# A written-out order of all queues replaced by another one, with four added dependencies of GpSimd on VectorE

## The chip, the core and the metric

The kernel runs on one core of one Trainium2 chip. Its time is the device time of one execution in microseconds (us), the median of the runs. The core has a matrix engine (TensorE, PE in the profile; its weight loads are PEld), a vector engine (VectorE, DVE), an engine for activation functions (ScalarE, ACT), a general engine (GpSimd, POOL) and a queue engine from which most transfers are started (SyncE, SP). Each engine works off its own list of instructions in order. Between engines an instruction waits on semaphores.

## The reference

```python
def attn(q, k, v, centroids):            # B=4, H=8, S=768, D=64; 16 centroids per head
    q_assign = argmax(normed(q) @ normed(centroids).T)      # a cluster for each query
    k_assign = argmax(normed(k) @ normed(centroids).T)      # and for each key
    mask = q_assign[:, :, :, None] == k_assign[:, :, None, :]
    scores = where(mask, (q @ k.T) / sqrt(D), -1e9)
    return softmax(scores) @ v
def moe(x, w_in, w_out, g_ln):           # x: 3072 x 512, w_in: 512 x 1024, w_out: 1024 x 512
    h = x @ w_in
    solu = h * softmax(h)
    ln = (solu - mean(solu)) / sqrt(var(solu) + 1e-6) * g_ln
    return ln @ w_out
out = moe(attn(...) as 3072 tokens x 512)
```

## The kernel before, in words

**Attention.** The tokens of q and k arrive by DMA (`ld`) and are turned so that the head's 64 dimensions lie on the partitions: for batch 0 by PE transposes with copies out of PSUM (`tp`, `xa`, `xt`), for batches 1 to 3 by transposes of VectorE (`xt`). Casts to bf16 (`ca`) write them into the operands `qbig` and `kbig`; casts of v are `cv`, blanks of `kbig` are `bl`. The clusters come from products with the centroids (`cl` on PE), which VectorE turns back (`tb`, line 479), reduces to a maximum (`mx`, line 489), compares with it (`oh`, line 493: 1 where the product is the maximum, else 0; its widest form has 768 columns and reads two tiles of SBUF) and turns again (`ot`, lines 500 and 505). Copies (`pl`, "place") write the rows so found as further contraction rows below q and k, so that a pair of one cluster gets a higher score and the exponential removes all others. Scores (`S`, line 641) come in 144 regions of 1024 columns, each of two halves; ScalarE exponentiates a region (`E`, line 651) into one of five tiles; `V` (line 663) multiplies with v and a column of ones into one PSUM bank (`ob`); `N` (lines 675 and 686) divides by that column on VectorE and writes x.

**FFN.** For each of 24 blocks f of 128 tokens: x is transposed (`tx`, a DMA; for the first and the last block `ptx` on PE with a copy), `h` (line 772) multiplies with w_in into two banks, `hm` (line 782, VectorE) copies out and keeps the maximum, `ex` (line 798) exponentiates, `u` (line 805) is the product h·e, on GpSimd or VectorE; `tu` transposes u (a DMA), `bn` and `ag` (lines 816, 821, 823) give its variance, `as` a small term of it, `al` (line 840, GpSimd) the factor alpha; `y` (line 844) multiplies with w_out into the one bank `mb`, `sc` (lines 856 on ScalarE, 858 on VectorE) scales it out with alpha and frees the bank for the next `y`, `ou` stores. `w_in` comes in four loads (`li`) with casts on GpSimd (`wi`, line 580); `lo`, `me`, `mf`, `ce` prepare w_out.

**Where the order comes from.** The kernel lists every step by name. The table `ORDER` is one list of all names; the steps are issued in that order, so that what stands in it for one engine is that engine's queue. The table `AWAY` names the engine of a step where it isn't the usual one. No scheduler moves anything afterwards; semaphores are put in for the data dependencies between engines. A name has the step, then its number: `S108.0` is the first half of region 108, `y10.0` the first quarter of block 10, `ca3.1.0.0` batch 3, pair 1, q, first half of the rows.

Of the kernel before, what the change touches and what calls it, by code (L numbers as in the profile page):

```python
# [23 lines left out]
""".split(), "ACT"))
AWAY.update(dict.fromkeys("""
    as0 as11 as14 as15 as17 as18 as19 as2 as22 as23 as4 as5 as9 bl1.2 bl3.0 ce0 ce2 ce4 km mk
    pl0.0.1.0.0 pl0.1.0.0 pl0.1.0.1 pl0.2.0.0 pl0.2.1.0 pl0.3.0.0 pl0.3.1.1 pl1.0.0.0
    pl1.2.0.0 pl2.0.0.0 pl2.0.0.1 pl2.0.1.1 pl2.2.0.0 pl3.0.0.1 pl3.2.0.1 pl3.2.1.0 sc0 sc1
    sc12 sc13 sc14 sc16 sc4 sc9
""".split(), "DVE"))  # L30
AWAY.update(dict.fromkeys("""
    ca0.0.0.0.0 ca0.0.0.0.1 ca0.0.0.1.0 ca0.0.0.1.1 ce1 ce3 pl0.0.1.1 u0.0 u1.0 u10.0 u11.0
    u12.0 u13.0 u15.0 u16.0 u17.0 u18.0 u19.0 u2.0 u21.0 u22.0 u3.0 u4.0 u5.0 u6.0 u7.0 u8.0
    u9.0
# [39 lines left out]
pl1.2.0.1 pl1.2.1.1 pl1.2.1.0 h4.0.1 as2 bl1.2 hm4.0 ag1 al0 u2.0 ca1.2.1.1 S53.0 S53.1 V33.0
V33.1 h4.1.0 xt2.0.0 sc0 h4.1.1 hm4.1 bn2.0 bn2.1 E52 E53 ex3.0 V34.0 S54.0 S54.1 S55.0 S55.1 E54
V34.1 V35.0 h5.0.0 h5.0.1 S56.0 S56.1 y1.0 E55 S57.0 S57.1 E56 cv1.2.0 V35.1 E57 y1.1 hm5.0 N15
tu2 ou0 ld2.2.0 ld2.2.1.0 ld2.2.1.1 y1.2 S58.0 S58.1 E58 h5.1.0 S59.0 S59.1 V36.0 V36.1 V37.0
V37.1 V38.0 S60.0 S60.1 h5.1.1 E59 E60 ex4.0 V38.1 y1.3 S61.0 S61.1 S62.0 S62.1 E61 E62 xt2.0.1
xt2.1.0 u3.0 ca2.0.0.1 ca2.0.0.0 al1 ag2 xt2.1.1 hm5.1 bn3.0 N16 bn3.1 cl2.1 cl2.0 tb2.1 ca1.3.1.0
cv1.2.1 ca1.3.0.0 as3 ag3 tb2.0 cv1.3.0 ca1.3.1.1 al2 u4.0 ca2.0.1.1 al3 ca2.1.0.0 ca2.1.1.0  # L80
cv1.3.1 V39.0 V39.1 S63.0 S63.1 S64.0 S64.1 V40.0 V40.1 sc1 V41.0 V41.1 y2.0 mx2.0 as4 N17 E63
S65.0 S65.1 E64 E65 y2.1 S66.0 S66.1 y2.2 y2.3 E66 tu3 tu4 ou1 ld2.2.1.2 ld2.2.1 S67.0 S67.1 V42.0
V42.1 S68.0 S68.1 V43.0 V43.1 sc2 oh2.0 ot2.0 N18 pl2.0.1.1 pl2.0.0.0 bn4.0 xt2.2.0 pl2.0.0.1
pl2.0.1.0 ca2.0.1.0 y3.0 E67 S69.0 S69.1 y3.1 ca2.2.0.1 bl2.0 E68 E69 S70.0 S70.1 E70 y3.2 V44.0
y3.3 V44.1 V45.0 S71.0 S71.1 S72.0 S72.1 V45.1 sc3 N19 tx6 y4.0 y4.1 E71 E72 S73.0 S73.1 E73 V46.0
# [12 lines left out]
ld3.2.0.0 ld3.2.0.1 ld3.2.0.2 ld3.2.0 tu7 ld3.2.1.0 ld3.2.1.1 ld3.2.1.2 ld3.2.1 bl2.2 al5 cv2.2.0
cv2.2.1 ca3.0.1.0 ca2.3.0.1 cl3.0 cl3.1 sc5 bn6.1 tb3.0 bn7.0 bn7.1 ag6 tb3.1 S93.1 S94.0 S94.1
V60.0 V60.1 V61.0 V61.1 y6.0 E93 E94 S95.0 S95.1 E95 h10.0.0 V62.0 V62.1 h10.0.1 h10.1.0 ex9.0  # L100
cv2.3.1 u8.0 S96.0 S96.1 E96 S97.0 N25 S97.1 E97 as7 y6.1 y6.2 V63.0 h10.1.1 as8 u9.0 ca3.0.0.1
ag7 bn8.0 hm10.0 S98.0 S98.1 S99.0 S99.1 h11.0.0 V63.1 V64.0 h11.0.1 E98 E99 S100.0 S100.1 E100
# [1252 lines left out]
```

## Time and profile before

| | |
|---|---|
| median of 3 runs | 222.03 us (221.85 to 222.12) |
| profiled execution | 222.33 us, its span 220.5 us |
| granted TensorE clock | 1.00 |
| busy: PE, ACT, DVE, POOL | 211.4, 192.8, 185.7, 158.8 us |
| HBM | 133 GB/s over the span |

A line of the profile gives the source line, engine, operation, output and input tiles and their shapes, then the count, the busy time in us and the mean of one in ns. The time after the second bar is how long the engine had been idle just before such instructions, and what ended it. "<-DVE y L858" means that the instruction's wait ended with that instruction of VectorE. In a timeline row the first two numbers are the start and the length. Some 1 to 3% of the matmul records are missing from the trace.

### The profile page before, as it was taken

Reading aid. Unit: us, or ns where it says so; the run is one execution under the profiler, and the core shown is the slowest. Engines: PE = TensorE matmul, PEld = TensorE weight load, DVE = VectorE, ACT = ScalarE, POOL = GpSimd, SP = SyncE. Lnnn points to the kernel's source line nnn. Section 1 sums busy time; section 2 is a strip of 40 time slices with the busy share of each in tenths; the row PEclk is TensorE's granted clock in tenths of the full one; section 3 lists DMA queues with packets and bytes.
Section 4 is the critical chain, followed back from the end, with each engine's and each line's share of the span. In section 5 each row is a group of like instructions: output and inputs, shape, how many; then the busy total and the mean of one; then the engine's idle time right before and its main releaser. Section 6 shows DMA issues by size and latency. Waiting matters only on the chain.

```text
span 220.5 us, 6292 instructions
## 1 busy us (share of the span) xinstructions
PE 211.4 (96%) x2401; PEld 148.9 (68%) x2431; DVE 185.7 (84%) x430; ACT 192.8 (87%) x245; POOL 158.8 (72%) x198
## 2 busy tenths in 40 slices
PE   7899999999999999999999999999999999999984
PEld 4567577677678776777677677666777767655442
DVE  3699979968999999896799999994888856989982
ACT  3799999999999998999999989999999888685362
POOL 3686969897898999549939997879889054456610
PEclk9999999999999999999999999999999999999999
DMA  5998999999999993999999981939584229777522
GB/s 199 394 402 259 189 175 300 126 154 259 164 154 169 190 188 62 174 248 210 153 225 162 180 184 38 171 92 209 151 173 90 72 64 168 154 120 170 163 94 100
DMA packets 120911, 38.33 MB, mean 174 GB/s; under 512 B 109993, under 2 KB 116401, under 8 KB 120881
## 3 DMA queue, kind: packets, MB, share of 16 engines
q1 hardware_dynamic: 120448, 37.40, 81.7%
q10 hardware_dynamic: 432, 0.52, 0.7%
q8 instruction: 19, 0.31, 0.6%
q14 instruction: 12, 0.09, 0.2%
HBM read 23.11 MB, written 6.29 MB: 133 GB/s over the span
## 4 chain that ended last, share of the span: by engine, by line
PE 72%; DVE 10%; DMA 6%; POOL 5%; issue 3%; ACT 2%; SPq 1%; DVEq 0%; ACTq 0%; POOLq 0%
PE sb L641 22%; PE hb L772 16%; PE mb L844 15%; PE ob L663 12%; DMA w_st<-in_moe_w_in_dram 4%; PE hb L470 3%; DMA raw<-in_q_dram 2%; DVE w_st L782 2%; PE hb L396 2%; DVE xt L421 2%; DVE bs L816 2%; POOL kbig L441 1%; PE mb L470 1%; POOL w_in_sb L580 1%; POOL v L556 1%
## 5 line engine op out<-in xcount | busy, mean ns | idle before, releaser
L651 ACT ACTIVATE e<-sb 128x1024 bf16<-128x1024 f32 x144 | 139.9, 1024 | 8.9 <-PE sb L641 8.1
L641 PE MATMUL sb<-qbig,kbig 80*128 80x256 bf16 (+3 forms) x648 | 83.8, 261 | 1.3 <-ACT e L651 1.0
L641 PEld LDWEIGHTS <-kbig 80*128 80x128 bf16 (+1 forms) x648 | 62.9, 119 | 25.4 <-issue 8.6
L805 POOL TENSOR_TENSOR u<-e_sb,w_st 128x1024 bf16<-128x1024 bf16 x21 | 45.1, 2145 | 20.0 <-ACT e_sb L798 13.3
L663 PEld LDWEIGHTS <-e 128*128 128x128 bf16 x1152 | 48.6, 97 | 10.4 <-DVE x L686 0.6
L663 PE MATMUL ob<-v,e 128*128 128x65 bf16 x1140 | 51.4, 193 | 0.2
L772 PE MATMUL hb<-w_in_sb,xT 128*128 128x512 bf16 x173 | 50.6, 379 | 0.9 <-POOL v L1323 0.3
L844 PE MATMUL mb<-w_out_c,uT 128*128 128x512 bf16 x165 | 45.5, 379 | 1.2 <-DVE y L858 0.4
L816 DVE BATCH_NORM_STATS2 bs<-u 128x6 f32<-128x512 bf16 x48 | 31.6, 680 | 1.1 <-POOL u L805 1.1
L798 ACT ACTIVATE e_sb<-w_st,nmax 128x1024 bf16<-128x1024 f32 (+1 forms) x25 | 27.8, 1113 | 3.2 <-DVE w_st L782 1.8
L439 POOL CAST qbig<-xt 64x768 bf16<-64x768 f32 (+1 forms) x31 | 25.7, 830 | 6.5 <-PE ob L663 2.7
L441 POOL TENSOR_SCALAR kbig<-xt 64x768 bf16<-64x768 f32 (+1 forms) x32 | 27.6, 865 | 2.4 <-DVE xt L409 0.8
L840 POOL TENSOR_TENSOR alpha<-var,halves 128x1 f32<-128x1 f32 x24 | 15.3, 638 | 12.6 <-DVE var L823 8.0
L421 DVE STREAM_TRANSPOSE xt<-raw 128x768 f32<-128x768 f32 x24 | 22.5, 959 | 0.1
L844 PEld LDWEIGHTS <-uT 128*128 128x128 bf16 x176 | 15.2, 97 | 10.2 <-issue 0.8
L772 PEld LDWEIGHTS <-xT 128*128 128x128 bf16 x192 | 15.8, 98 | 8.8 <-issue 0.6
L686 DVE TENSOR_TENSOR x<-ob,den 128x256 bf16<-128x256 f32 (+2 forms) x40 | 19.0, 474 | 1.4
L782 DVE TENSOR_SCALAR_CACHE_REDUCE w_st<-hb 128x512 f32<-128x512 f32 x24 | 16.3, 680 | 3.8 <-PE hb L772 3.7
L782 DVE TENSOR_SCALAR_CACHE_REDUCE w_st<-hb,nmax 128x512 f32<-128x512 f32 x24 | 17.8, 740 | 1.9 <-PE hb L772 1.5
L856 ACT ACTIVATE y<-mb,alpha 128x512 f32<-128x512 f32 x15 | 10.3, 685 | 6.5 <-POOL alpha L840 3.6
L675 DVE RECIPROCAL den<-ob 128x4 f32<-128x4 f32 (+2 forms) x40 | 7.1, 178 | 10.4 <-PE ob L663 10.1
L556 POOL CAST v<-vf 128x384 bf16<-128x384 f32 x22 | 10.9, 504 | 3.3 <-DMA vf<-in_v_dram 2.6
(109 smaller groups left out, 202.6 us busy)
## 6 DMA issues: line engine op xcount, KB each, us to landing
vf<-in_v_dram SPq DMA_DIRECT2D x16, 384.0 KB, 5.3
out_dram<-y SPq DMA_DIRECT2D x23, 256.0 KB, 2.5
...
```

What stands on the lines that cost most here:

```text
L421: nc.vector.transpose(xts[b, p, i][:], raw_of(b, p, i))
L439: (nc.vector if e == "DVE" else nc.gpsimd).tensor_copy(dst, src)
L441: (nc.vector if e == "DVE" else nc.gpsimd).tensor_scalar(dst, src, scalar1=inv_C, scalar2=1.0, op0=Alu.mult, op1=Alu.mult)
L641: nc.tensor.matmul(reg[:, c:c + wd], kb[u, pp, side_of(h), keys], qb[u, pp, side_of(h), su * P:su * P + wd])
L651: nc.scalar.activation(es[r][:, :w], src, Act.Exp, scale=exp_scale, bias=-exp_scale)
L663: nc.tensor.matmul(ops_of(group_of[n])[:, s, :VW], es[r][:, c0:c0 + P], v1[index[b, pair_of(h)] % R][:, side_of(h), kt, :VW], start=(kt == ...
L772: nc.tensor.matmul(hb[f2][:], xTs[f][:, dc, :], w_in_sb[:, dc, f2 * BANK:(f2 + 1) * BANK], start=(dc == 0), stop=(dc == n_dc - 1))
L782: nc.vector.tensor_scalar(ff[f, "h"][:, f2 * BANK:(f2 + 1) * BANK], hb[f2][:], scalar1=-1.0, scalar2=nmax[:, f2 - 1:f2] if f2 else 3.0e38, ...
L798: nc.scalar.activation(ff[f, "e"][:, cols(f, f2)], ff[f, "h"][:, cols(f, f2)], Act.Exp, bias=ff[f, "nmax"][:, n_ff2 - 1:], scale=-1.0, acc ...
L805: (nc.vector if e == "DVE" else nc.gpsimd).tensor_tensor(ff[f, "u"][:, cols(f, f2)], ff[f, "e"][:, cols(f, f2)], ff[f, "h"][:, cols(f, f2) ...
L816: nc.vector.bn_stats(ff[f, "bs"][:, f2, :], ff[f, "u"][:, f2 * BANK:(f2 + 1) * BANK])
L844: nc.tensor.matmul(y_of(f, x), ff[f, "uT"][:, fc, :], w_out_c[:, fc, parts_of(f, x)], start=(fc == 0), stop=(fc == n_fc - 1))
```

## The change

ORDER is another list of the same steps: the queue of every engine is in another order, those of the DMA queue too. AWAY moves some steps to another engine: seven from GpSimd to ScalarE, eleven from ScalarE to GpSimd, 24 from VectorE to GpSimd (u14.0 and u20.0 among them), 20 from GpSimd to VectorE (u10.0, u13.0, u16.0, bl1.0 and bl3.2 among them), pl0.1.1.1, sc3, sc11 and sc15 from ScalarE to VectorE, pl3.2.1.0, sc12, sc13, sc14 and sc16 the other way. What each step computes, the tiles and the number of PE instructions stay. `BEHIND` is new: a step of GpSimd waits until a step of VectorE has ended, though no data pass between them.

```diff
 AWAY.update(dict.fromkeys("""
-    ca0.0.1.1.0 ca0.2.0.1 ca1.0.0.1 ca3.1.1.0 ca3.2.0.1 cv0.0.1 cv0.1.0 cv0.2.1 cv1.2.0
...
+    ca0.0.1.0.0 ca0.2.0.1 ca1.0.0.1 cv0.1.0 cv0.1.1 cv0.2.0 cv1.2.0 cv2.0.1 cv3.0.0 cv3.1.1
...
 """.split(), "ACT"))
...
 ORDER = """
...
-V46.1 S74.0 S74.1 E74 y4.2 y4.3 V47.0 lv2.0 ou2 ld3.0.0.0 lv2.1 tx8 lv2.2 ex5.0 V47.1 S75.0 S75.1
...
+V45.1 y4.1 E70 E71 S72.0 S72.1 E72 S73.0 S73.1 bn4.0 N19 V46.0 V46.1 V47.0 V47.1 bn4.1 y4.2 S74.0
...
 """.split()
+BEHIND = dict(x.split(":") for x in """
+    al3:oh2.0 al5:oh2.2 u9.0:oh3.0 ca3.1.0.0:oh3.2
+""".split())
...
-    def run(self):
-        done, holder = set(), {}
+    def run(self, tc):
+        done, holder, last = set(), {}, {}
         for name in ORDER:
...
+            block = tc.nc.cur_bb.bb
+            n = len(block.instructions)
             o["fn"]()
+            if name in BEHIND or name in BEHIND.values():
+                new = list(block.instructions)[n:]
+                last[name] = new[-1].name
+            if name in BEHIND:
+                tc.add_manual_dep(new[0], last[BEHIND[name]], mybir.DependencyInfo(
+                    mybir.DependencyClass.Sync, mybir.DependencyReason.DATA), reason="behind")
             done.add(name)
```

All lines of the steps have numbers higher by 13 after the change, in the rows below too.

VectorE, around sc1, the copy of the second y block (`y` from `mb`), before; `bs` are bn3.0 and bn3.1, `cst` tb2.1 and tb2.0, `mv` and `var` ag3, `den` and `x` N16:

```order
L782 TENSOR_SCALAR w_st_1504,nmax_1505<-hb1_93,nmax_1505 128x512
L816 BN_STATS bs_1611<-u_1598 128x6
L675 RECIPROCAL den_1613<-ob_94 128x6
L686 TENSOR_TENSOR x_1185<-ob_94,den_1613 128x6x64
L816 BN_STATS bs_1611<-u_1598 128x6
L479 STREAM_TRANSPOSE cst_1625<-hb1_93 128x384
L821 BN_AGGR mv_1632<-bs_1611 128x2
L823 TENSOR_SCALAR var_1634<-es6_1630,esum_1444,mv_1632 128x1
L479 STREAM_TRANSPOSE cst_1625<-hb0_92 128x384
L858 TENSOR_SCALAR y_1681<-mb_95,alpha_1602 128x512
```

The same place after the change (`mv` and `var` ahead of N16 are ag2):

```order
L795 TENSOR_SCALAR w_st_1496,nmax_1497<-hb1_93,nmax_1497 128x512
L834 BN_AGGR mv_1615<-bs_1428 128x2
L836 TENSOR_SCALAR var_1617<-es6_1302,esum_1273,mv_1615 128x1
L688 RECIPROCAL den_1619<-ob_94 128x6
L699 TENSOR_TENSOR x_1190<-ob_94,den_1619 128x6x64
L871 TENSOR_SCALAR y_1622<-mb_95,alpha_1432 128x512
L848 TENSOR_SCALAR es6_1670<-esum_1410 128x1
L829 BN_STATS bs_1506<-u_1435 128x6
```

sc1 stands directly behind N16; bn3.1, both tb and ag3 have moved behind it.

VectorE around sc9, before: it follows N30, bn10.1 and ot3.2.

```order
L675 RECIPROCAL den_2912<-ob_94 128x6
L686 TENSOR_TENSOR x_2911<-ob_94,den_2912 128x6x64
L816 BN_STATS bs_2730<-u_2716 128x6
L500 STREAM_TRANSPOSE oht_2990<-oh_2850 128x768
L858 TENSOR_SCALAR y_2992<-mb_95,alpha_2780 128x512
```

After (the first row is hm14.0, `es6` as12, the memset bl3.2, `bs` bn11.0 and bn11.1, the `mv` ag9, ag10 and ag11):

```order
L795 TENSOR_SCALAR w_st_2908,nmax_2909<-hb0_92 128x512
L848 TENSOR_SCALAR es6_2911<-esum_2875 128x1
L556 MEMSET kbig1_100 16x2x384
L829 BN_STATS bs_2929<-u_2902 128x6 x2
L834 BN_AGGR mv_2932<-bs_2807 128x2
L836 TENSOR_SCALAR var_2934<-es6_2630,esum_2434,mv_2932 128x1
L834 BN_AGGR mv_2938<-bs_2812 128x2
L836 TENSOR_SCALAR var_2940<-es6_2783,esum_2708,mv_2938 128x1
L834 BN_AGGR mv_2947<-bs_2929 128x2
L836 TENSOR_SCALAR var_2949<-es6_2900,esum_2777,mv_2947 128x1
L829 BN_STATS bs_2951<-u_2915 128x6
L871 TENSOR_SCALAR y_3027<-mb_95,alpha_2936 128x512
```

ot3.2 stands further ahead now, and nine instructions of the statistics and a memset stand between hm14.0 and sc9.

GpSimd after the change, from u9.0 on (the first row; its wait on DVE is that for oh3.0); behind it ca3.1.1.1, ca3.0.0.0, al6, pl3.0.1.1, pl3.0.0.1, ca3.1.1.0, cv3.0.1, ca3.0.1.0, pl3.0.0.0, al7 and al8, and after these rows as9 and pl3.0.1.0, the last that S108.0 needs:

```order
L818 TENSOR_TENSOR u_2500<-e_sb_2435,w_st_2247 128x1024 [waits DMAHW5_49,DVE_49,Activation_49]
L454 TENSOR_SCALAR kbig0_99<-xt_2258 64x768 [waits PE_49,Pool_49]
L452 CAST qbig0_96<-xt_2252 64x768
L853 TENSOR_TENSOR alpha_2504<-var_2491,halves_126 128x1 [waits Pool_49]
L544 COPY kbig0_99<-oht_2509 32x4x192 [waits DVE_49,Pool_49]
L544 COPY qbig0_96<-oht_2509 32x4x192
L454 TENSOR_SCALAR kbig0_99<-xt_2258 64x768 [waits Pool_49]
L569 CAST v1_0_102<-vf_2269 128x6x64 [waits DMAHW5_49]
L454 TENSOR_SCALAR kbig0_99<-xt_2254 64x768
L544 COPY qbig0_96<-oht_2509 32x4x192 [waits Pool_49]
L853 TENSOR_TENSOR alpha_2626<-var_2608,halves_126 128x1 [waits DVE_49,Pool_49]
L853 TENSOR_TENSOR alpha_2628<-var_2618,halves_126 128x1 [waits DVE_49]
```

The same place before: u9.0 is the fourth row, and the placings (L531) come later.

```order
L805 TENSOR_TENSOR u_2442<-e_sb_2314,w_st_2099 128x1024 [waits DMAHW6_49,Activation_49]
L835 TENSOR_SCALAR es6_2459<-esum_2143 128x1
L835 TENSOR_SCALAR es6_2473<-esum_2313 128x1
L805 TENSOR_TENSOR u_2475<-e_sb_2439,w_st_2305 128x1024 [waits DMAHW0_49,DVE_49,Activation_49]
L439 CAST qbig0_96<-xt_2308 64x768 [waits PE_49,Pool_49]
L840 TENSOR_TENSOR alpha_2541<-var_2375,halves_126 128x1 [waits DVE_49,Pool_49]
L556 CAST v1_5_107<-vf_2330 128x6x64
L439 CAST qbig0_96<-xt_2321 64x768 [waits PE_49,Pool_49]
L840 TENSOR_TENSOR alpha_2545<-var_2480,halves_126 128x1 [waits DVE_49,Pool_49]
L439 CAST qbig0_96<-xt_2308 64x768
L441 TENSOR_SCALAR kbig0_99<-xt_2319 64x768 [waits Pool_49]
L531 COPY qbig0_96<-oht_2607 32x4x192 [waits DVE_49]
```

The first placing stands eight rows behind u9.0 before and four rows behind it after, and u9.0 has the wait for oh3.0 now.

VectorE in the tail, before, from hm21.0 to N39 (`u` is u20.0, the `bs` bn19.1, bn20.0, bn20.1):

```order
L782 TENSOR_SCALAR w_st_3779,nmax_3780<-hb0_92 128x512
L782 TENSOR_SCALAR w_st_3779,nmax_3780<-hb1_93,nmax_3780 128x512
L821 BN_AGGR mv_3783<-bs_3626 128x2
L823 TENSOR_SCALAR var_3785<-es6_3715,esum_3582,mv_3783 128x1
L805 TENSOR_TENSOR u_3800<-e_sb_3744,w_st_3717 128x1024
L816 BN_STATS bs_3752<-u_3681 128x6
L816 BN_STATS bs_3807<-u_3800 128x6 x2
L675 RECIPROCAL den_3810<-ob_94 128x2
L686 TENSOR_TENSOR x_2911<-ob_94,den_3810 128x128
```

After:

```order
L795 TENSOR_SCALAR w_st_3780,nmax_3781<-hb0_92 128x512
L795 TENSOR_SCALAR w_st_3780,nmax_3781<-hb1_93,nmax_3781 128x512
L829 BN_STATS bs_3799<-u_3670 128x6
L848 TENSOR_SCALAR es6_3801<-esum_3733 128x1
L829 BN_STATS bs_3799<-u_3670 128x6
L829 BN_STATS bs_3826<-u_3821 128x6 x2
L688 RECIPROCAL den_3829<-ob_94 128x2
L699 TENSOR_TENSOR x_2893<-ob_94,den_3829 128x128
```

u20.0 and ag18 are gone from between; bn19.0 has come behind hm21.1.

More of the change, by code (lines that the diff above doesn't have):

```diff
@@ L24 @@
 """.split(), "ACT"))
 AWAY.update(dict.fromkeys("""
[L26 to L29, printed above, removed]
+    as1 as10 as12 as13 as15 as16 as17 as20 as23 as3 as5 as6 as7 as8 bl1.0 bl1.2 bl3.2 ce0 ce2
+    ce4 km mk pl0.0.1.0.0 pl0.0.1.1.0 pl0.1.1.1 pl0.2.1.1 pl0.3.0.0 pl0.3.1.1 pl1.0.0.1
@@ L74 @@
[L74 to L85, printed above, removed]
@@ L98 @@
[L98 to L102, printed above, removed]
-V64.1 V65.0 V65.1 mx3.0 al6 cv2.3.0 ca3.1.0.1 al7 ca3.0.0.0 ca3.0.1.1 hm10.1 h11.1.0 oh3.0 hm11.0
@@ new lines @@
+S110.0 S110.1 V70.1 V71.0 V71.1 E109 E110 ex11.0 hm12.0 as10 oh3.2 y8.0 h12.1.1 y8.1 ca3.3.0.1
+bl3.0 ca3.3.1.0 S111.0 S111.1 S112.0 S112.1 N29 bn9.0 bn9.1 u10.0 bn10.0 hm12.1 bn10.1 y8.2 y8.3
+V72.0 V72.1 V73.0 h13.0.0 E111 E112 S113.0 S113.1 S114.0 S114.1 V73.1 h13.0.1 h13.1.0 h13.1.1
+V74.0 ot3.2 cv3.1.1 sc8 ex12.0 E113 hm13.0 V74.1 y9.0 h14.0.0 N30 hm13.1 ca3.1.0.1 ca3.1.0.0 as11
+u11.0 h14.0.1 E114 hm14.0 as12 pl3.2.1.0 pl3.2.1.1 u12.0 ca3.3.0.0 tu10 ou7 tx16 lv3.2 ou8 tu11
+bl3.2 bn11.0 bn11.1 ag9 al9 ag10 al10 pl3.2.0.0 cv3.1.0 ca3.2.0.0 ag11 bn12.0 ca3.2.1.0 ca3.2.1.1
@@ new lines @@
+h21.0.1 y17.0 y17.1 y17.2 hm20.1 ex20.0 S141.0 S141.1 E141 h21.1.0 y17.3 S142.0 S142.1 h21.1.1
+S143.0 S143.1 sc17 as18 ag18 as19 al18 hm21.0 hm21.1 E142 E143 ex21.0 y18.0 V94.0 bn19.0 as20
+y18.1 V94.1 y18.2 h22.0.0 h22.0.1 y18.3 sc18 u20.0 u21.0 bn19.1 bn20.0 bn20.1 N39 ag19 ag20 hm22.0
+h22.1.0 V95.0 V95.1 h22.1.1 hm22.1 ex22.0 al19 as21 u22.0 y19.0 ptx23.0 tx23.0 N40 y19.1 y19.2
+y19.3 ptx23.1 h23.0.0 h23.1.0 ou17 tu20 ou18 tu21 bn21.0 tx23.1 bn21.1 al20 h23.0.1 sc19 y20.0
+y20.1 y20.2 y20.3 sc20 h23.1.1 ou19 hm23.0 ag21 bn22.0 hm23.1 ptu22.0 ptu22.1 tu22.1 bn22.1 ex23.0
```

187 lines of the change are left out of this document (97 added, 90 removed).

## The prediction

> **What bounds the kernel now.** I read the page first, then the busy times by stage, then the waits, then the chain that ended last, and last the single stretches in which TensorE (PE) stands still.
>
> ```profile
> span 220.5 us, 6292 instructions
> PE 211.4 (96%) x2401; PEld 148.9 (68%) x2431; DVE 185.7 (84%) x430; ACT 192.8 (87%) x245; POOL 158.8 (72%) x198
> 0.00:14.00 14.00, 12.07 (x79) 7.39 (x80) 7.90 (x29) 8.70 (x18) 7.92 (x30) 1.00 0.87 318
> 14.00:44.00 30.00, 28.57 (x383) 20.07 (x383) 26.88 (x54) 29.32 (x36) 24.35 (x33) 1.00 1.00 226
> 44.00:204.00 160.00, 158.13 (x1861) 114.73 (x1886) 139.56 (x316) 147.71 (x181) 121.57 (x131) 1.00 0.84 157
> 204.00:221.00 17.00, 12.63 (x87) 6.75 (x85) 11.38 (x34) 7.08 (x14) 4.98 (x7) 1.00 0.36 116
> ```
>
> The stage rows give length, then the busy time of PE, PEld, DVE, ACT and POOL. From 44 to 204 us PE is busy 158.13 of 160 us: 1.87 us can be won there, and anything that makes PE wait is lost. From 14 to 44 us ACT stands beside it (29.32 of 30). The clock is 1.00 throughout, so nothing is won there.
>
> ```profile
> L641 PE MATMUL sb<-qbig,kbig 80*128 80x256 bf16 (+3 forms) x648 | 83.8, 261 | 1.3 <-ACT e L651 1.0
> ACT e L651 <- PE sb L641: 8.1, 19, 1.1
> 108.14 1.43 PE hb L470 x16
> 161.03 0.88 PE sb L641 x8
> 208.14 1.74 PE mb L844 x8
> ```
>
> PE waits 1.0 us in all for ACT's exponentials, ACT waits 8.1 us for PE's scores: PE leads. Three steps of the chain that ended last, from middle to end, say the same: they are PE work. PE's instructions are as many after the change as before, so the time is decided by the few gaps of PE that go, come or grow. The sum is made against the profiled execution, 222.33 us (span 220.5 and 1.8 around it), which lies 0.30 above the median of 222.03; I take 0.30 off at the end.
>
> **The change part by part.** First the gaps that go.
>
> ```profile
> 84.83 0.89 PE L663 MATMUL ob<-v,e 128*128 128x65 bf16 x24
> 85.32 0.71 DVE L858 TENSOR_SCALAR y<-mb,alpha 128x512 f32<-128x512 f32 x1
> 86.08 0.38 PE L844 MATMUL mb<-w_out_c,uT 128*128 128x512 bf16 x1 [0.36 <-DVE y L858]
> L816 DVE BATCH_NORM_STATS2 bs<-u 128x6 f32<-128x512 bf16 x48 | 31.6, 680 | 1.1 <-POOL u L805 1.1
> L479 DVE STREAM_TRANSPOSE cst<-hb 128x384 f32<-128x384 f32 x12 | 6.8, 577 | 0.5 <-PE hb L470 0.2
> L821 DVE BATCH_NORM_AGGREGATE mv<-bs 128x2 f32<-128x12 f32 x24 | 4.7, 195 | 0.1
> L823 DVE TENSOR_SCALAR var<-es,esum,mv 128x1 f32<-128x1 f32 x23 | 6.3, 273 | 1.4
> ```
>
> T1. There is one PSUM bank for y, so y2.0 waits for sc1, the copy of y1: 0.36 us by the row, about 0.5 against PE's usual start-to-start spacing. Between N16 and sc1 DVE now does bn3.1, two tb and ag3; after the change sc1 stands directly behind N16. By the rows 0.68 + 2×0.58 + 0.20 + 0.27 = about 2 us earlier. PE also has 6.0 us of work between y1.3 and y2.0 instead of 4.4 (two S halves, two V and two h more). The gap goes: −0.45 (0 to −0.5).
>
> ```profile
> 41.72 1.04 POOL L580 CAST w_in_sb<-w_st 128x1024 bf16<-128x1024 f32 x1 [0.80 <-DMA w_st<-in_moe_w_in_dram]
> 41.89 0.59 PE L772 MATMUL hb<-w_in_sb,xT 128*128 128x512 bf16 x2
> 42.81 0.38 PE L772 MATMUL hb<-w_in_sb,xT 128*128 128x512 bf16 x1 [0.33 <-POOL v L1323]
> 10.37 0.88 PE L396 MATMUL hb<-ident_f,raw 128*128 128x128 f32 x6 [0.26 <-ACT v L554]
> ```
>
> T2. h0.0.1 waits for the last cast of w_in on GpSimd (41.72 to 42.76), which waits for its DMA. The same bytes are queued ahead of that DMA afterwards, so I let it land at the same time; one V group (0.18 us) is put between on PE: −0.25 (0 to −0.5). T3. At the start the loads of pair 2 go ahead of the first load of v, and the wait at 10.37 goes; the next transpose then waits for ACT's copy xt0.1.0 instead: −0.1 (0 to −0.3).
>
> Now the gaps that come. All durations on DVE are means of the groups, less 0.08 for each neighbour, because successive vector instructions overlap (three statistics take 1.87, not 3×0.68).
>
> ```profile
> 201.02 1.87 DVE L816 BATCH_NORM_STATS2 bs<-u 128x6 f32<-128x512 bf16 x3
> L782 DVE TENSOR_SCALAR_CACHE_REDUCE w_st<-hb,nmax 128x512 f32<-128x512 f32 x24 | 17.8, 740 | 1.9 <-PE hb L772 1.5
> L858 DVE TENSOR_SCALAR y<-mb,alpha 128x512 f32<-128x512 f32 x8 | 5.9, 736 | 1.8 <-POOL alpha L840 1.2 <-PE mb L844 0.7
> L500 DVE STREAM_TRANSPOSE oht<-oh 128x768 bf16<-128x768 bf16 x6 | 5.8, 971 | 0.1
> 199.88 1.22 DVE L805 TENSOR_TENSOR u<-e_sb,w_st 128x1024 bf16<-128x1024 bf16 x1
> 205.40 0.29 DVE L686 TENSOR_TENSOR x<-sb,den 128x128 bf16<-128x128 f32 x1
> 205.98 0.22 PE L747 MATMUL sb<-ident_b,x 128*128 128x128 bf16 x1
> ```
>
> T4. y10.0 waits for sc9. Before, sc9 stands behind ot3.2; now behind bl3.2, bn11.0, bn11.1, ag9, ag10, ag11 and bn12.0, and u10.0 (1.22) has come to DVE ahead of it. From hm12.0 through sc9 I sum on DVE: five hm 3.2, oh and ot 1.9, two N 1.4, seven bn 4.2, u 1.1, three ag 1.35, bl and as 0.8, sc 0.7 = 14.7 us; plus 0.5 in which hm14.0 must wait for its matmuls. PE has 15.15 us of work from h12.0.1 to y10.0 (20 S halves at 0.22, 14 V at 0.18, 19 h and y at 0.43). That is even, so semaphore steps decide: +0.25 (0 to 0.7, one bn).
>
> T5. In the tail ptx23.1 needs N40. Before, N40 ends at 205.69 and ptx23.1 starts at 205.98: no wait. Afterwards DVE does between h21.1.1 and the end of N40: hm21.1 0.7, four bn 2.4, as 0.1, N39 0.4, two ag 0.9, two hm 1.3, tx23.0 0.3, N40 0.5, and links, 6.7 us; PE has 6.5. u20.0 is on GpSimd now (2.15 for 1.22), and bn20.0 may wait for it. +0.25 (0 to 0.85). T6. cl3.3 waits for the last of four DVE transposes, now behind hm11.1: +0.15 (0 to 0.7, one hm).
>
> T7. ACT gets lighter.
>
> ```profile
> L437 ACT ACTIVATE qbig<-xt 64x768 bf16<-64x768 f32 x3 | 2.5, 842 | 0.1
> L554 ACT CAST v<-vf 128x384 bf16<-128x384 f32 x10 | 5.1, 512 | 0.1
> L856 ACT ACTIVATE y<-mb,alpha 128x512 f32<-128x512 f32 x15 | 10.3, 685 | 6.5 <-POOL alpha L840 3.6 <-PE mb L844 2.9
> ```
>
> Two whole casts and two casts of v fewer (2×0.84 + 2×0.51), one copy of y more (0.69): −2.0 us on ACT. Nearly all of it lies after E25, where PE leads, so it is hidden behind PE; it can only take from the 1.0 us in which PE waits for E. I take −0.3 (0 to −1.0). DVE changes by about −2.8, GpSimd by about +5.3, mostly beside PE work.
>
> **The four dependencies.** Each holds a GpSimd step until a wide compare (oh) of VectorE has ended.
>
> ```profile
> 86.90 0.55 POOL L840 TENSOR_TENSOR alpha<-var,halves 128x1 f32<-128x1 f32 x1
> 87.40 0.82 POOL L439 CAST qbig<-xt 64x768 bf16<-64x768 f32 x1
> 87.56 1.48 DVE L493 TENSOR_TENSOR oh<-cst,mx 128x768 bf16<-128x768 f32 x1
> 88.19 1.53 POOL L441 TENSOR_SCALAR kbig<-xt 64x768 bf16<-64x768 f32 x1
> 111.78 0.95 DVE L493 TENSOR_TENSOR oh<-cst,mx 128x768 bf16<-128x768 f32 x1
> L805 POOL TENSOR_TENSOR u<-e_sb,w_st 128x1024 bf16<-128x1024 bf16 x21 | 45.1, 2145 | 20.0 <-ACT e_sb L798 13.3 <-issue 5.6 <-DVE y L858 0.6
> L441 POOL TENSOR_SCALAR kbig<-xt 64x768 bf16<-64x768 f32 (+1 forms) x32 | 27.6, 865 | 2.4 <-DVE xt L409 0.8
> L531 POOL COPY kbig<-oht 32x768 f32<-32x768 f32 (+2 forms) x14 | 10.0, 712 | 2.4 <-DVE oht L505 1.0 <-PE sb L641 0.5 <-DVE oht L500 0.3
> ```
>
> The compare at 87.56 began under a cast of GpSimd and took 1.48 us, one without it took 0.95; the next cast began under the compare and took 1.53 instead of 0.82. So one collision costs each side 0.5 to 0.7 us. The Trainium skill ("SBUF — State Buffer", section "SBUF: two separate sides") calls this an exclusive lock: a vector operation with two SBUF inputs or a GpSimd operation, whichever starts first, keeps the port pair for the whole instruction. The trace agrees (0.53 lost with 0.66 of the cast left). By that rule alone a u9.0 that began just before oh3.0 would hold it for about 2 us, and the dependencies would be a gain of that size on DVE, none of it on PE while slack remains.
>
> By the rows: u9.0 could begin about 1.8 us before oh3.0 ends and is held so long. Queued behind it on GpSimd up to S108.0 are four casts (3.4), al6, al7, al8 (0.55 each), four placings (3.3), a cast of v (0.5), an as (0.2), with u9.0 itself 2.15: 11.1 us. PE has about 12.1 us from the end of oh3.0 to S108.0. One microsecond is spare: 0 in the forecast (0 to +1.2). The al3 before S72.0 has about as much; al5 and ca3.1.0.0 more.
>
> Sum: −0.45 −0.25 −0.1 +0.25 +0.25 +0.15 −0.3 = −0.45, so 222.33 − 0.45 − 0.30 = 221.6. The tail from y20.0 on (12.5 us) keeps its two structural waits and its length.
>
> **The rivals.** A, the forecast: gains and new waits nearly cancel, 221.0 to 222.2; 0.39.
>
> B, the small waits of PE go almost everywhere. For it: ACT is 2 us lighter, and PE idles 1.87 us from 44 to 204 and 1.43 from 14 to 44. Against it: from E0 to E25 ACT's sum is unchanged. T1 to T3 at their ends (−1.3), half of what else is idle after 44 (−0.5), T4 to T6 at zero: 222.03 − 1.8 = 220.2 at best, 220.7 likely; 0.18.
>
> C, slower: GpSimd becomes late in one place, u9.0 to S108.0. It decides when oh3.0 ends over 1 us later than I sum, or two of the thirteen steps queued there run into wide vector operations at 0.5 to 0.7 each. For it: GpSimd carries 5 us more, and the wait puts a whole u behind DVE's clock. Then S108.0 stops PE for 0.5 to 1.5 us, and E behind it: 221.6 + 1.0 = 222.6, up to 223.4; 0.25.
>
> D, PE is not full. The Trainium skill ("Perfetto Trace Analysis", section "Identifying the Most-Contended Engine") calls matmul busy time a bad measure of headroom and takes weight-load time; here that is 68%, below ACT's 87%. As a mechanism here: the matmuls would close up wherever ACT frees a bank earlier, and the time would follow ACT's −2.0: 220.0. Against it stands ACT's 8.1 us of waits for PE; 0.06.
>
> E, slower: DVE is late at both sc9 and N40 (T4 and T5 at their upper ends, +1.05 over the forecast): 222.6; 0.12.
>
> **How the numbers follow.** 221.6 is that of A. The range holds A, most of B, C and E: 220.4 to 223.4. A measurement of this kernel can tell about 0.2% (0.44 us) from no change: faster means below 221.59, slower above 222.47. A is split evenly: 0.20 faster, 0.19 the same. With B and D faster has 0.44; same 0.19; slower 0.37 from C and E.
>
> **What would show it.** Right: y2.0 and h0.0.1 without idle time before them; y10.0 and ptx23.1 idle at most 0.5 us, with DVE named; S108.0 without a wait; oh3.0 and oh2.0 near 0.95 us. Wrong: S72.0 or S108.0 waiting for a GpSimd copy (C); y10.0 or ptx23.1 late by 0.7 or more (E); PE busy above 159 of 160 us in the middle (B); or a stall at a place not named here, which would mean that my sums of the queues miss a wait.

## The result, and the profile after

The changed kernel takes 223.41 us (median, 223.08 to 224.36) where the kernel before takes 222.03 (221.43 to 222.16): ratio 1.0072, 95% interval 1.0053 to 1.0091. It is slower by 0.7%, just above the forecast range. The trace below is of an execution of 223.08 us, 0.75 longer than the profiled one of before.

The page and the busy times by stage of the changed kernel (length, then PE, PEld, DVE, ACT, POOL):

```profile
span 221.3 us, 6294 instructions
PE 213.2 (96%) x2431; PEld 147.8 (67%) x2431; DVE 182.0 (82%) x425; ACT 191.0 (86%) x242; POOL 160.7 (73%) x206
0.00:14.00 14.00, 11.43 (x79) 6.69 (x80) 7.66 (x28) 8.38 (x17) 8.53 (x30) 1.00 0.89 312
14.00:44.00 30.00, 28.98 (x400) 20.50 (x399) 26.86 (x54) 29.21 (x35) 26.44 (x35) 1.00 0.98 241
44.00:204.00 160.00, 159.48 (x1866) 113.52 (x1865) 135.42 (x309) 146.01 (x178) 119.00 (x134) 1.00 0.83 155
```

ACT and DVE got lighter, about as worked out (192.8 to 191.0, 185.7 to 182.0); GpSimd rose by 1.9 us and not by 5.3. But PE is busier in the middle than before and the kernel is slower: busy shares don't settle this. The count in brackets says why. Here PE has as many matmul records as weight loads (2431); before it had 2401 (1.2% fewer), so some of its 1.87 us of "idle" in the middle were records that the trace had lost.

What works is to follow PE's delay: the start of a PE step, less the sum of the usual start-to-start spacings of all PE steps ahead of it in the queue (half of a region S 0.216 us, V 0.182, h and y 0.432, cl 0.77). The sum of the spacings is the "PE work done". The delay grows where PE really waits. It also grows a little where spacings are slightly above the usual ones (0.4 us from 48 to 78, with no wait of note), so columns are to be compared with each other. Growth per stretch, in us, worked out from the PE rows of four traces; "again" and "mended" are runs told of below:

| us of PE work done | before | changed | changed again | mended | what waits |
|---|---|---|---|---|---|
| 0 to 12 | 3.05 | 3.06 | 2.99 | 2.92 | the start |
| 12 to 24 | 0.94 | 0.60 | 0.60 | 0.60 | S behind E |
| 24 to 30 | 1.63 | 1.59 | 2.37 | 1.59 | S behind E; ptx0, cl1.0 |
| 30 to 36 | 0.84 | 0.59 | 0.52 | 0.58 | before: h0.0.1 (T2) |
| 36 to 48 | 0.16 | 0.98 | 0.98 | 0.39 | cl1.2 |
| 48 to 78 | 0.38 | 0.41 | 0.41 | 0.61 | |
| 78 to 84 | 0.55 | 0.02 | 0.01 | 0.02 | before: y2.0 (T1) |
| 84 to 144 | 0.40 | 0.30 | 0.31 | 0.31 | cl3.3 (T6) |
| 144 to 150 | 0.05 | 0.95 | 0.94 | 0.11 | S118.0, y10.0 (T4) |
| 150 to 192 | 0.19 | 0.18 | 0.35 | 0.37 | |
| 192 to 198 | 0.01 | 0.34 | 0.35 | 0.00 | ptx23.1 (T5) |
| 198 to the end | 1.13 | 1.06 | 1.06 | 1.06 | the tail |
| sum | 9.33 | 10.08 | 10.89 | 8.56 | |

The two gains that were forecast came: y2.0 and h0.0.1 start without a wait in the changed kernel's timeline, right behind the rows ahead of them.

```profile
42.19 0.35 PE L676 MATMUL ob<-v,e 128*128 128x65 bf16 x6
42.38 0.59 PE L785 MATMUL hb<-w_in_sb,xT 128*128 128x512 bf16 x2
...
84.03 0.50 PE L676 MATMUL ob<-v,e 128*128 128x65 bf16 x11
84.37 0.59 PE L857 MATMUL mb<-w_out_c,uT 128*128 128x512 bf16 x2
```

Waits that before did not have, at three places, took more than that back. The first place, in the timeline of the changed kernel around cl1.2 (L483):

```profile
51.50 0.43 DVE L699 TENSOR_TENSOR x<-ob,den 128x256 bf16<-128x256 f32 x1
52.14 0.70 DVE L556 MEMSET kbig<- 16x768 f32 x1 [0.21 <-issue]
52.87 0.98 DVE L434 STREAM_TRANSPOSE xt<-raw 128x768 f32<-128x768 f32 x1
53.25 1.49 PE L483 MATMUL hb<-xt,c_bd 128*32 128x384 f32 x8
```

The memset is bl1.0, which came to VectorE from GpSimd. It stands ahead of xt1.2.1, whose transpose ends at 53.85; cl1.2 starts at 53.25, needs it for its second half, and takes 1.49 us instead of 0.85. The wait lies inside the group's duration, where no bracket names it.

The second place has two waits, at S118.0 (L654) and y10.0 (L857):

```profile
152.47 0.83 ACT L542 COPY kbig<-oht 32x768 f32<-32x768 f32 x1
152.83 0.15 DVE L848 TENSOR_SCALAR es<-esum 128x1 f32<-128x1 f32 x1
153.59 0.70 DVE L556 MEMSET kbig<- 16x768 f32 x1 [0.61 <-ACT kbig L542]
156.58 0.60 PE L654 MATMUL sb<-qbig,kbig 80*128 80x256 bf16 x4 [0.15 <-ACT e L664]
157.37 0.73 DVE L871 TENSOR_SCALAR y<-mb,alpha 128x512 f32<-128x512 f32 x1
158.16 0.59 PE L857 MATMUL mb<-w_out_c,uT 128*128 128x512 bf16 x2 [0.37 <-DVE y L871]
```

The placing pl3.2.1.0 went from VectorE to ScalarE (152.47 to 153.30). The blank bl3.2 must follow it, so VectorE stands idle 0.61 us and sc9 ends at 158.11. On ScalarE the same copy delays E116, and S118.0 waits for that. The third place is ptx23.1 (L760) in the tail, which waits for N40 (L699):

```profile
206.88 0.29 DVE L699 TENSOR_TENSOR x<-sb,den 128x128 bf16<-128x128 f32 x1
207.23 0.23 PE L760 MATMUL sb<-ident_b,x 128*128 128x128 bf16 x1 [0.17 <-DVE x L699]
```

### The profile page after: what moved, and what is told of

Same layout as the page of the kernel before. It is cut to its first block, busy times and chain, and to the rows that moved or that the text cites. A ratio compares the mean times of both kernels' runs of the same rounds, so it can differ in the third digit from the quotient of the medians.

```text
span 221.3 us, 6294 instructions
## 1 busy us (share of the span) xinstructions
PE 213.2 (96%) x2431; PEld 147.8 (67%) x2431; DVE 182.0 (82%) x425; ACT 191.0 (86%) x242; POOL 160.7 (73%) x206
## 4 chain that ended last, share of the span: by engine, by line
PE 74%; ACT 13%; DVE 5%; issue 3%; DMA 2%; POOL 1%; SPq 1%; DVEq 0%; POOLq 0%; ACTq 0%
PE sb L654 23%; PE hb L785 16%; PE mb L857 14%; PE ob L676 13%; ACT e L664 10%; PE hb L483 4%; DMA raw<-in_q_dram 2%; DVE bs L829 2%; ACT e_sb L811 2%; PE hb L409 1%; DVE w_st L795 1%; POOL u L818 1%; ACT xt L420 1%; PE mb L483 1%; DVE y L871 1%
## 5 line engine op out<-in xcount | busy, mean ns | idle before, releaser
L654 PE MATMUL sb<-qbig,kbig 80*128 80x256 bf16 (+3 forms) x648 | 81.2, 261 | 1.2 <-ACT e L664 1.0
L654 PEld LDWEIGHTS <-kbig 80*128 80x128 bf16 (+1 forms) x648 | 63.0, 119 | 25.4 <-issue 9.6
L818 POOL TENSOR_TENSOR u<-e_sb,w_st 128x1024 bf16<-128x1024 bf16 x20 | 42.9, 2144 | 17.8 <-ACT e_sb L811 13.1
L676 PEld LDWEIGHTS <-e 128*128 128x128 bf16 x1152 | 48.0, 97 | 9.8 <-issue 0.8
L785 PE MATMUL hb<-w_in_sb,xT 128*128 128x512 bf16 x192 | 52.7, 379 | 0.0
L676 PE MATMUL ob<-v,e 128*128 128x65 bf16 x1140 | 50.7, 193 | 0.0
L857 PE MATMUL mb<-w_out_c,uT 128*128 128x512 bf16 x176 | 48.3, 379 | 0.6 <-DVE y L871 0.4
L853 POOL TENSOR_TENSOR alpha<-var,halves 128x1 f32<-128x1 f32 x24 | 14.1, 592 | 17.1 <-DVE var L836 14.7
L857 PEld LDWEIGHTS <-uT 128*128 128x128 bf16 x176 | 14.6, 97 | 10.3 <-issue 1.0
L699 DVE TENSOR_TENSOR x<-ob,den 128x256 bf16<-128x256 f32 (+2 forms) x40 | 19.0, 474 | 1.4
L544 POOL COPY qbig<-oht 32x768 f32<-32x768 f32 (+1 forms) x15 | 11.5, 768 | 5.3 <-DVE oht L513 4.5
L869 ACT ACTIVATE y<-mb,alpha 128x512 f32<-128x512 f32 x16 | 11.0, 690 | 4.9 <-POOL es L848 2.5
```

The costliest lines, as they stand in the source:

```text
L654: nc.tensor.matmul(reg[:, c:c + wd], kb[u, pp, side_of(h), keys], qb[u, pp, side_of(h), su * P:su * P + wd])
L676: nc.tensor.matmul(ops_of(group_of[n])[:, s, :VW], es[r][:, c0:c0 + P], v1[index[b, pair_of(h)] % R][:, side_of(h), kt, :VW], start=(kt == ...
L785: nc.tensor.matmul(hb[f2][:], xTs[f][:, dc, :], w_in_sb[:, dc, f2 * BANK:(f2 + 1) * BANK], start=(dc == 0), stop=(dc == n_dc - 1))
L818: (nc.vector if e == "DVE" else nc.gpsimd).tensor_tensor(ff[f, "u"][:, cols(f, f2)], ff[f, "e"][:, cols(f, f2)], ff[f, "h"][:, cols(f, f2) ...
L857: nc.tensor.matmul(y_of(f, x), ff[f, "uT"][:, fc, :], w_out_c[:, fc, parts_of(f, x)], start=(fc == 0), stop=(fc == n_fc - 1))
```

## Experiments

Delays in what follows are PE's, by the method of the table; times are medians, ratios to the kernel before on the same chip.

**The changed kernel again**, unaltered.

> The changed kernel once more, unaltered, for a second trace and a second interval. Its first trace was 0.75 us longer than that of the kernel before, its median 1.4 us longer. Theory 1 (three fixed waits of PE: 0.75 us in cl1.2 for the transpose xt1.2.1, 0.85 us at S118.0 and y10.0 behind the placing pl3.2.1.0, 0.33 us at ptx23.1 for N40): the second trace shows the same three waits, within 0.1 us each, and the ratio is again about 1.006. Theory 2 (the extra time is in waits for DMA that come and go from run to run): the second trace has its waits at other places, and the three above are smaller or gone.

Measured 223.90 us, ratio 1.0061 (1.0033 to 1.0089). The waits stand at the same three places, with 0.98, 0.94 and 0.35 us of delay. Theory 1 holds and theory 2 falls as the cause of these. But there is a fourth wait, 0.78 us between 24 and 30 us of PE work, that the first trace did not have. The timeline of the changed kernel, first trace (L631 is ce0 and ce2 on VectorE, L635 and L637 ce6 on GpSimd, the den at 34.22 the start of N5, L739 ptx0):

```profile
32.55 1.75 DVE L631 SCALAR_TENSOR_TENSOR w_out_c<-w_g,g_ln,y 128x512 bf16<-128x512 f32 x2
34.22 0.17 DVE L688 RECIPROCAL den<-ob 128x4 f32<-128x4 f32 x1
...
32.53 1.23 POOL L635 TENSOR_SCALAR w_g<-w_g,g_ln 128x512 f32<-128x512 f32 x1
33.85 1.58 POOL L637 TENSOR_TENSOR w_out_c<-w_g,y 128x512 bf16<-128x512 f32 x1
...
35.09 0.61 PE L739 MATMUL hb<-ident_b,x 128*128 128x128 bf16 x8
```

The same rows of the second trace:

```profile
32.48 2.82 DVE L631 SCALAR_TENSOR_TENSOR w_out_c<-w_g,g_ln,y 128x512 bf16<-128x512 f32 x2
35.22 0.17 DVE L688 RECIPROCAL den<-ob 128x4 f32<-128x4 f32 x1
...
32.39 0.69 POOL L635 TENSOR_SCALAR w_g<-w_g,g_ln 128x512 f32<-128x512 f32 x1
33.16 1.58 POOL L637 TENSOR_TENSOR w_out_c<-w_g,y 128x512 bf16<-128x512 f32 x1
...
35.90 0.51 PE L739 MATMUL hb<-ident_b,x 128*128 128x128 bf16 x6 [0.61 <-DVE x L699]
```

With GpSimd 0.09 us ahead, its first instruction takes 0.69 us and VectorE's two take 2.82. With 0.02 us between them, GpSimd's takes 1.23 and VectorE's two take 1.75. N5 is then 1.0 us earlier, and ptx0 does not wait for it. Of the six traces of kernels with these steps unaltered (first, again, and the next three runs and the one without dependencies) five have the 2.8 us. The first trace was the lucky one; that is a part of why it was only 0.75 us longer than that of before, where the medians differ by 1.4.

**xt1.2.1 ahead of bl1.0**

```diff
-... hm1.0 xt1.2.0 N10 bl1.0 xt1.2.1 E34 ...
+... hm1.0 xt1.2.0 N10 xt1.2.1 bl1.0 E34 ...
```

> The changed kernel with one swap on VectorE: xt1.2.1 ahead of bl1.0. Theory 1: the last four products of cl1.2 no longer wait, cl1.2 takes 0.85 us instead of 1.49, the wait before S39.0 goes, and the time is 0.6 to 0.75 us below that of the changed kernel (222.7 where that has 223.4). Rival: ScalarE, which stands beside PE there, or the scores that need bl1.0 take the place of the wait, and the gain is under 0.3 us.

Measured 223.59 us, ratio 1.0055 (1.0033 to 1.0078), 0.3 below the run beside it, with intervals that overlap. The trace tells more (cl1.2 is L478 here, V24.0 the last row):

```profile
54.09 0.85 PE L478 MATMUL hb<-xt,c_bd 128*32 128x384 f32 x8
54.88 1.08 PE L649 MATMUL sb<-qbig,kbig 80*128 80x256 bf16 x8
55.96 0.51 PE L671 MATMUL ob<-v,e 128*128 128x65 bf16 x11
```

cl1.2 takes 0.85 us. PE's delay between 36 and 48 us of work falls from 0.98 to 0.34; 0.18 of that comes back at V24.0, which waits for N11, now behind bl1.0. Net 0.46 in the trace: the mechanism of the theory holds, with a smaller gain than expected, and the time alone would not show it.

**The placing pl3.2.1.0 on GpSimd**

```diff
-    cv3.3.1 pl0.0.0.0 pl0.0.0.1 pl1.2.1.0 pl3.2.1.0 xa0.0.0 ...   # to ScalarE
+    cv3.3.1 pl0.0.0.0 pl0.0.0.1 pl1.2.1.0 xa0.0.0 ...            # the usual engine, GpSimd
```

> The changed kernel with the placing pl3.2.1.0 on GpSimd instead of ScalarE. Theory 1: the blank bl3.2, which must follow the placing, starts about 0.6 us earlier on VectorE, sc9 and y10.0 with it, and E116 comes 0.8 us earlier, so both waits go: PE gains 0.7 to 0.9 us (222.6). Rival (the order of VectorE alone, as my term T4 had it, makes y10.0 late by 0.25 to 0.5 us): y10.0 keeps a wait of 0.25 us or more and the gain is 0.3 to 0.6 us.

**The blank bl3.2 on GpSimd**, the placing still on ScalarE

```diff
-    as1 as10 ... as8 bl1.0 bl1.2 bl3.2 ce0 ...   # to VectorE
+    as1 as10 ... as8 bl1.0 bl1.2 ce0 ...         # the usual engine, GpSimd
```

> The changed kernel with the blank bl3.2 on GpSimd, as in the kernel before, and the placing pl3.2.1.0 still on ScalarE. This tells the two waits apart. Theory 1: the wait of VectorE for the placing (0.6 us) and the blank itself (0.7 us) leave the queue ahead of sc9, so y10.0 loses its wait of 0.53 us; the wait of 0.3 us at S118.0 for E116 stays, since ScalarE still does the placing: gain 0.5 us (222.9). Rival (both waits come from VectorE): both go, gain 0.8 us or more; or (both come from ScalarE) neither goes.

Measured 223.10 (1.0054, 1.0023 to 1.0085) and 223.43 (1.0048, 1.0025 to 1.0072). y10.0 and what is ahead of it, first with the placing moved:

```profile
153.47 0.70 DVE L556 MEMSET kbig<- 16x768 f32 x1 [0.20 <-issue]
157.25 0.74 DVE L871 TENSOR_SCALAR y<-mb,alpha 128x512 f32<-128x512 f32 x1
158.04 0.59 PE L857 MATMUL mb<-w_out_c,uT 128*128 128x512 bf16 x2 [0.28 <-DVE y L871]
```

and with the blank moved (S118.0 is the first row):

```profile
157.08 0.60 PE L655 MATMUL sb<-qbig,kbig 80*128 80x256 bf16 x4 [0.15 <-ACT e L665]
157.51 0.35 PE L677 MATMUL ob<-v,e 128*128 128x65 bf16 x6
157.70 0.59 PE L786 MATMUL hb<-w_in_sb,xT 128*128 128x512 bf16 x2
158.13 0.59 PE L858 MATMUL mb<-w_out_c,uT 128*128 128x512 bf16 x2
```

With the placing moved S118.0's wait goes, but y10.0 keeps 0.44 us: PE gets there sooner, and VectorE's queue ahead of sc9 (memset, three statistics, three ag) is too long by itself. There the rival was right and theory 1 wrong. With the blank moved y10.0's wait goes and S118.0's 0.31 stays, as theory 1 had it. So S118.0 is ScalarE's copy, and y10.0 is VectorE's queue, lengthened by the blank. The traces decide this; the medians lie 0.8 and 0.5 us below the run beside them, with intervals too wide to tell one theory from the other.

**ce2 on GpSimd**, in its idle time

```diff
-... li2 ce0 ce2 N5 ptx0 ...        # ce2 on VectorE
+... ca1.0.1.1 ce2 ...              # ce2 on GpSimd
```

> The changed kernel with one step moved: ce2 (line 631 on VectorE, two inputs in SBUF) goes to GpSimd, into its idle time behind ca1.0.1.1. In four traces out of five of the changed kernel and its variants ce0 and ce2 took 1.1 and 1.75 us beside ce6 of GpSimd, N5 began at 35.2 instead of 34.2 us, ptx0 took 1.40 us instead of 0.61 and cl1.0 1.14 instead of 0.85: PE lost 0.7 us more between 28 and 36 us than in the one trace where VectorE went first. Theory 1 (the two engines shut each other out, and which goes first decides): with ce2 gone N5 starts within 0.3 us of V11.1's end every time, ptx0 takes 0.61, and the time is 0.6 to 0.8 us below the changed kernel's 223.4 to 223.9. Rival (the x of N5 is late because V11.1 is late, or ptx0 waits for something else): ptx0 keeps 1.4 us and the time stays.

Measured 223.17, ratio 1.0043 (1.0027 to 1.0058). N5 starts at 33.72, behind the end of V11.1, ptx0 takes 0.61 us, and the delay between 24 and 30 us of work is 1.60 instead of 2.37: the expected 0.7 us. The times show less, a ratio of 1.0043 against 1.0061 for the unaltered kernel (0.4 us), with intervals that overlap.

**A fifth dependency, ce6 behind ce2**

```diff
-    al3:oh2.0 al5:oh2.2 u9.0:oh3.0 ca3.1.0.0:oh3.2
+    al3:oh2.0 al5:oh2.2 u9.0:oh3.0 ca3.1.0.0:oh3.2 ce6:ce2
```

> The changed kernel with a fifth dependency of the change's own kind: ce6 on GpSimd waits until ce2 on VectorE has ended; queues and engines unaltered. It tests what decides the wait at ptx0 without taking ce2 away. Theory 1 (who starts first holds the other up): ce0 takes 0.74 and ce2 about 1.1 us as in the first trace of the changed kernel, N5 follows V11.1 within 0.3 us, ptx0 takes 0.61 us, and PE wins 0.7 us against the four slow traces (total near 222.9); GpSimd pays with ce6, ce1 and wi2, wi1, wi3 about 1.5 us later, and h0.0.1, which needs them, may wait 0.5 us. Rival (ce0 and ce2 are slow whatever GpSimd does, by their own operands): ce2 keeps 1.75 us and the time stays.

Measured 223.11, ratio 1.0042 (1.0029 to 1.0056). The rows of its timeline:

```profile
32.43 1.41 DVE L631 SCALAR_TENSOR_TENSOR w_out_c<-w_g,g_ln,y 128x512 bf16<-128x512 f32 x2
...
33.99 0.69 POOL L635 TENSOR_SCALAR w_g<-w_g,g_ln 128x512 f32<-128x512 f32 x1 [1.62 <-PE sb L654]
34.77 1.27 POOL L637 TENSOR_TENSOR w_out_c<-w_g,y 128x512 bf16<-128x512 f32 x1
...
34.97 0.61 PE L739 MATMUL hb<-ident_b,x 128*128 128x128 bf16 x8
```

Alone, ce0 and ce2 take 0.74 and 0.75 us, together 1.41 (2.82 beside GpSimd). The delay from 24 to 30 is 1.59, and h0.0.1 does not pay for the later casts. This settles the cause: the same instructions, the same order, only the overlap gone. In time it is again about 0.4 us. The Trainium skill ("SBUF — State Buffer", section "SBUF: two separate sides") says that a VectorE operation with two SBUF inputs and a GpSimd operation that reads SBUF lock each other out for a whole instruction, whichever starts first. The durations agree; "first" does not quite, since with GpSimd 0.02 us ahead in the record VectorE went first. So close, the record may not tell the order.

**Without the four dependencies**

```diff
-BEHIND = dict(x.split(":") for x in """
-    al3:oh2.0 al5:oh2.2 u9.0:oh3.0 ca3.1.0.0:oh3.2
-""".split())
+BEHIND = {}
```

> The changed kernel without its four dependencies (BEHIND empty), the same order. My prediction: nothing on PE, since about a microsecond is spare at S72.0 and S108.0; oh3.0 or u9.0, and oh2.0 or al3, collide again and one of each pair takes 0.4 to 2 us longer; the time stays within 0.2 us. Rival 1 (the dependencies cost time): the time falls by 0.3 us or more. Rival 2 (the lock without them holds a wide compare for a whole u, 2 us, over the spare microsecond): S108.0 or S72.0 waits and the time rises by 0.3 us or more.

Measured 223.73, ratio 1.0067 (1.0048 to 1.0087), against 1.0061 with them. Three of the collisions come back, and GpSimd bears them; it starts second at two of them and level with VectorE at the third. u9.0 and oh3.0 in the timeline without the dependencies:

```profile
127.78 0.95 DVE L504 TENSOR_TENSOR oh<-cst,mx 128x768 bf16<-128x768 f32 x1
...
128.38 2.36 POOL L816 TENSOR_TENSOR u<-e_sb,w_st 128x1024 bf16<-128x1024 bf16 x1 [0.99 <-ACT e_sb L809]
```

u9.0 takes 2.36 us instead of 2.14 (ca3.1.0.0 1.63 instead of 0.82, al3 1.19 instead of 0.55). At oh2.2 nothing changes: two alphas of GpSimd take 1.77 us together with and without the dependency of al5. PE's delay from 84 to 144 us of work is 0.30 in both. The dependencies neither cost nor bring anything that these runs show.

**The waits mended together**: the swap of xt1.2.1, ce2, pl3.2.1.0 and bl3.2 on GpSimd, and ag20 behind N40

```diff
-... N39 ag19 ag20 hm22.0 ... tx23.0 N40 y19.1 ...
+... N39 ag19 hm22.0 ... tx23.0 N40 ag20 y19.1 ...
```

> The changed kernel with the four waits found so far mended together: xt1.2.1 ahead of bl1.0, ce2, pl3.2.1.0 and bl3.2 on GpSimd, and ag20 behind N40 on VectorE. Theory 1 (the waits are fixed and independent): 0.45 (cl1.2, net of the wait of V24.0) + 0.7 (ptx0 and cl1.0) + 0.85 (S118.0 and y10.0) + 0.3 (ptx23.1) = 2.3 us below the changed kernel's 223.5, 221.2, and so 0.8 us below the kernel before. Rival (PE is held by something else as soon as these go, such as ScalarE's exponentials or a DMA): half of that or less, no better than the kernel before (222.0).

Measured 221.28 us (220.84 to 221.76), ratio to the kernel before 0.9957 (0.994 to 0.9974): theory 1 to 0.1 us. The table gives 10.89 − 8.56 = 2.33 us less delay than in the changed kernel's second trace. With ag20 behind N40 the wait at ptx23.1 is gone. This kernel beats both others. In its rows of stages PE is busy 159.92 of 160 us from 44 to 204.

```profile
14.00:44.00 30.00, 28.99 (x399) 20.54 (x399) 26.17 (x54) 29.23 (x35) 26.51 (x35) 1.00 0.99 240
44.00:204.00 160.00, 159.92 (x1880) 113.88 (x1878) 136.31 (x312) 145.55 (x178) 123.07 (x137) 1.00 0.83 156
```

**The same with cv0.1.1 on GpSimd**

```diff
-    ca0.0.1.0.0 ca0.2.0.1 ca1.0.0.1 cv0.1.0 cv0.1.1 cv0.2.0 ...   # to ScalarE
+    ca0.0.1.0.0 ca0.2.0.1 ca1.0.0.1 cv0.1.0 cv0.2.0 ...
```

> The mended kernel of the earlier run with one more step moved: cv0.1.1 from ScalarE to GpSimd, between ca0.3.1.1 and pl0.3.1.0, where GpSimd idles 0.44 us. PE waits 1.7 us in all for E10 to E20 between 26 and 36 us, where ScalarE is full. If ScalarE's sum bounds that stretch, PE wins 0.5 us and the time is 220.8; rival: V7.0, which needs the cast, or the placing behind it takes the place, and the time stays at 221.3.

Measured 221.31, ratio 0.9971 (0.9955 to 0.9988): no gain over the mended kernel. PE's waits at S16.0 and S19.0 keep their 0.48 us each; ScalarE's sum in that stretch is not what holds them, and what does is open. By the method of the table a wait of 0.35 us at S22.0 goes and one of 0.09 comes at S24.0; the times are too coarse to show that.

**The kernel before with sc1 directly behind N16**

```diff
-... bn3.0 N16 bn3.1 ... tb2.0 ... V40.0 V40.1 sc1 V41.0 V41.1 y2.0 ...
+... bn3.0 N16 sc1 bn3.1 ... tb2.0 ... V40.0 V40.1 V41.0 V41.1 y2.0 ...
```

> The kernel before with one step moved: sc1 directly behind N16 on VectorE, as in the changed kernel (term T1 alone). Expected: the wait at y2.0 (0.53 us against PE's usual spacing) goes, the time falls by 0.45 us (0.3 to 0.5), to 221.6. Rival: another wait takes its place (sc1 ahead of tb2.1 and tb2.0 delays oh2.0 and so S72.0) and the time stays. Its trace is also a second look at all other waits of the kernel before: by theory 1 they are the same as in the first, within 0.1 us each, with no wait of 0.7 us between 28 and 36 us, since there ce0 and ce5 stand apart.

Measured 222.01, ratio 0.9998 (0.9979 to 1.0017): too wide for an effect of 0.2%. In the trace y2.0's wait is gone (0.03 us of delay instead of 0.55 between 78 and 84 us of work), but 0.26 comes back up to 102 us of work, where the kernel before gains 0.10 and this one 0.36. T1 alone is worth about 0.25, not 0.45. Its stage row has all records of PE:

```profile
44.00:204.00 160.00, 160.00 (x1889) 114.68 (x1886) 139.94 (x318) 147.79 (x181) 121.64 (x130) 1.00 0.84 157
```

## Why the prediction was wrong

The frame held: the number of PE instructions is the same, PE leads, and the time is the sum of its gaps. The sign was wrong: 221.6 was forecast, 223.41 measured. The last of its own signs of being wrong came true: stalls at places that it does not name, cl1.2 and ptx0. The steps that failed are T4, which was mis-sized, and two moves that it put at nothing: bl1.0 ahead of xt1.2.1, and ce0 and ce2 beside ce6.

- T1's wait went as forecast: −0.45, and −0.53 in the table, though alone on the kernel before it brought about 0.25.
- T2's size came out (−0.25; −0.25 to −0.3 in the table), its reason did not. The last cast of w_in ends at 40.46 us instead of 42.76, where the prediction let its data land at the same time. Nor is that wait fixed: in the other trace of the old order, the one with sc1 moved, h0.0.1 waits only about 0.1 us. T3 brought 0 for −0.1; the next transpose waits for xt0.1.0, as the term itself said.
- T5 (+0.25) and T6 (+0.15) measured +0.33 and about 0.05.
- T7 (−0.3) agrees with a gain of 0.34, but by luck: that gain lies at 12 to 24 us of work, and ACT's busy time from 14 to 44 us hardly fell (29.32 to 29.21). A cast of q stands at 24.44 in ACT's queue before and at 21.38 after, so a better order is the likely cause; no run tests it. After 44 us, where the work went, "it is hidden behind PE" was right.
- T4 failed in size: +0.25 forecast, +0.9 measured. With the placing taken off ScalarE, y10.0 is still 0.44 us late behind VectorE's queue, so the sum of VectorE against PE was about 0.2 short by itself. The rest is the placing that the change moved to ScalarE. The sum took the blank as 0.7 us of work and not as a step that waits for that placing (0.61 us idle). And the placing's 0.83 us on ScalarE was counted in the sum of the engine (−2.0) but not where it falls, ahead of E115 to E118: S118.0, 0.3 us.
- Two terms were missing. bl1.0's move to VectorE was one of twenty from GpSimd that I took, all but a few, as lying beside PE work. The delay around cl1.2 grew by 0.8 us, of which the swap won 0.46 back; the rest is not accounted for. And ce0 and ce2, put together on VectorE against ce6 on GpSimd: 0.7 us in five traces of six. (In time, taking it away won about 0.4.) I had measured the price of a collision (0.5 to 0.7 us each) and then looked for it only at the four places that the change itself names.
- The four dependencies cost nothing, as forecast, and C did not happen: pl3.0.1.0 ends at 139.78 and S108.0 starts at 140.57, 0.79 us spare where 1.0 was worked out. E named the right mechanism, VectorE late at sc9 and N40; by the table these two cost 1.2 us, cl1.2 and the collision 1.5, against gains of 1.3 (y2.0, h0.0.1, the 0.34 at 12 to 24 and small ones).
- B rested on 1.87 us of PE idle time in the middle. That number was mostly lost records: another trace of the kernel before's order, with sc1 moved, shows 160.00 busy of 160. PE's count of matmuls beside its count of weight loads (1861 and 1886) would have said so.
- D fell: ACT lost 1.8 us of work and the time rose. Where the trace has all its records, matmul busy time said rightly that PE is full (159.92 of 160 us in the mended kernel), but not that it never waits. One product of y is recorded with 0.38 us and the next can start 0.216 after it, so a short wait disappears under the record. From 44 to 204 us the changed kernel shows 0.52 us without matmuls, where cl1.2, S118.0 and y10.0 alone waited 0.64 + 0.31 + 0.53 us. The prediction's 1.0 us of PE waiting for E was short in the same way: S12.0, S16.0 and S19.0 of the kernel before start 0.48 us late each.
